# Seven products for the first dense matrix, with its factors streamed from DRAM

## The chip, the cores and the metric

One core of one Trainium2 chip. The time is the device time of one execution in microseconds (us); three runs give a median. A profile of one more execution tells what each engine did.

## The reference

q, k, v are [8, 8, 576, 64]; a decayed causal attention turns them into 4608 tokens of 512 features. A mixture of eight experts follows (each token goes to its best expert: 512 to 1024, relu, 1024 to 512, times its gate). Last comes the dense part, which the change is about:

```python
def _moe2_ref(x, w_in, w_out):      # x 4608 x 512, w_in 512 x 2048, w_out 2048 x 512
    h = x @ w_in
    r = np.maximum(h, 0.0)
    g = r * r
    return (g @ w_out).astype(np.float32)
```

## The kernel before

Matrices are multiplied on TensorE in three terms: each operand is split into a high part and a low rest (`hi`, `lo`), and hi x hi, hi x lo and lo x hi are added in PSUM. A split is a copy on ScalarE (the high part) and a subtraction on VectorE (the rest).

Three stages follow one another. The attention takes the first 200 us or so. The expert part runs over 64 units, eight for each expert, 640 slots an expert: `first(u + 1)` makes 128 hidden features of unit u + 1 (24 matmuls of 320 columns in two halves, whose relu is ScalarE's L718 and whose rest is VectorE's L719), then `second(u)` adds unit u to five accumulators (15 matmuls of 512 columns). While TensorE does this the other engines do, in the order in which the loop over units (L860 on) writes them: SyncE loads the weights seven units ahead, SyncE puts a split of dense weights into DRAM, ScalarE and VectorE split the weights of unit u + 6 (L97, L98; GpSimd does the subtraction in one unit of eight), GpSimd gathers the next expert's tokens, VectorE turns them (L684) and splits them (L689). The dense weights come as 64-bit words. `split_wide` (L127 to L146) takes 512 columns of them apart with seven operations on VectorE and two on ScalarE, five times in eight units; `cw_p` has two buffers for the result, and the transfer to `wd_d` in DRAM is issued two units later. Engines work through their queues in the written order.

The dense part (L916 on) goes over nine blocks of 512 tokens. All 16 tiles of split weights (1 MB each) lie in SBUF: four are loaded late in the expert part, twelve at its end. A step (block b, feature tile f) is `up`: 12 matmuls into one bank; `squares`: relu, square, split, for the step after next; `down`: 12 matmuls of the squares into four accumulators. `fetch` reads a block's rows from `y_d`, `turn` turns and splits them during the block before. The first block begins in halves of 256 columns, since its third and fourth tiles of tokens are scattered to DRAM by the last expert while it starts.

## Time and profile before

| what | value |
|---|---|
| median of 3 runs | 1429.58 us (1426.47 to 1435.66) |
| the profiled execution | 1436.04 us, its span 1434.2 us |
| TensorE busy | 1391.3 us, 97% of the span |
| VectorE, ScalarE, GpSimd busy | 712.5, 435.3, 313.2 us |
| mean granted clock of TensorE | 0.991 of 2.4 GHz |
| mean rate of all transfers | 120 GB/s |

The span runs from the first to the last instruction; the profiled execution's own time is 1.8 us longer. The busy time of an engine is a sum over stages with different limits; the tables by stretch say where it falls. A wait is put down to the signal that came last.

### The profile page before, as it was taken

To read this page: it belongs to the slowest core of one execution; us is meant where nothing else is said; L and a number is where in the kernel's file an instruction comes from. 1 tells how busy PE (TensorE), PEld (TensorE's weight loads), DVE (VectorE), ACT (ScalarE), POOL (GpSimd) and SP (SyncE) were. 2 spreads that over 40 slices of the span, in tenths; PEclk is the share of its full clock that TensorE was granted. 3 is DMA by queue.
4 is the path that set the end of the run, shared out by engine and by line. 5 is a ranking of instruction groups with operands and counts; after the bars stand their busy time and mean duration, and the time that the engine had idled before them with its cause. 6 is when DMAs were issued, how large, how long until landed. Compare 5 with 4: busy or idle time off the path is not lost.

```text
span 1434.2 us, 20323 instructions
## 1 busy us (share of the span) xinstructions
PE 1391.3 (97%) x8217; PEld 1192.2 (83%) x8217; DVE 712.5 (50%) x1187; ACT 435.3 (30%) x764; POOL 313.2 (22%) x277
## 2 busy tenths in 40 slices
PE   7989799998999999999999999999999999999998
PEld 5777688887999999998888888888888888888887
DVE  5667656886888888723323233232333323333222
ACT  1212233443444444422222222222222222222221
POOL 2223246765657557310000000000000000000000
PEclk9999999999999999999999999999999999999999
DMA  8999744765756757538120020200102020020000
GB/s 309 293 298 303 210 131 135 241 226 176 234 186 222 227 185 237 189 134 312 81 59 0 1 59 0 59 1 27 33 0 59 1 57 3 0 59 1 30 0 30
DMA packets 92406, 172.51 MB, mean 120 GB/s; under 512 B 16654, under 2 KB 54030, under 8 KB 86672
## 3 DMA queue, kind: packets, MB, share of 16 engines
q1 hardware_dynamic: 82944, 151.03, 33.3%
q0 software_dynamic: 9360, 20.10, 4.3%
q8 instruction: 66, 1.08, 0.3%
q14 instruction: 36, 0.29, 0.1%
HBM read 125.86 MB, written 46.28 MB: 120 GB/s over the span
## 4 chain that ended last, share of the span: by engine, by line
PE 72%; issue 3%; DMA 1%; POOL 0%; SPq 0%; ACT 0%; POOLq 0%; DVE 0%
PE fl L937 27%; PE fa L959 9%; PE fa L958 9%; PE fa L960 9%; PE l L712 3%; PE l L713 3%; PE l L714 3%; PE acc L737 3%; PE acc L736 3%; PE acc L738 3%; DMA w<-wd_d 1%; DMA y_d<-y,sidx 0%; POOL y_d L227 0%; SPq L633 0%; DMA yi<-y_d 0%
## 5 line engine op out<-in xcount | busy, mean ns | idle before, releaser
L937 PE MATMUL fl<-xt,w 128*128 128x512 f32 (+1 forms) x1776 | 415.3, 383 | 1.5 <-DMA w<-wd_d 1.5
L937 PEld LDWEIGHTS fl<-xt,w 128*128 128x128 f32 x1776 | 327.1, 188 | 67.3 <-issue 1.9
L944 DVE TENSOR_TENSOR fr<-fr 128x512 f32<-128x512 f32 x144 | 99.8, 693 | 401.2 <-ACT fr L942 401.2
L958 PE MATMUL fa<-w,gh 128*128 128x512 f32 x576 | 224.1, 389 | 0.0
L959 PE MATMUL fa<-w,gh 128*128 128x512 f32 x576 | 224.1, 389 | 0.0
L960 PE MATMUL fa<-w,gl 128*128 128x512 f32 x576 | 224.1, 389 | 0.0
L942 ACT ACTIVATE fr<-fl 128x512 f32<-128x512 f32 x144 | 86.2, 599 | 416.0 <-PE fl L937 416.0
L206 POOL DMA_INDIRECT xs<-x_d,qidx x140 | 154.0, 1100 | 44.4 <-issue 42.4
L712 PE MATMUL l<-xt,w 128*128 128x320 f32 (+1 forms) x480 | 150.2, 313 | 8.8 <-DVEq L759 6.2
L713 PE MATMUL l<-xt,w 128*128 128x320 f32 (+1 forms) x480 | 149.8, 312 | 0.0
L948 DVE TENSOR_TENSOR gl<-fr,gh 128x512 fp32r<-128x512 f32 x144 | 99.8, 693 | 100.6 <-ACT gh L946 100.6
L714 PE MATMUL l<-xt,w 128*128 128x320 f32 (+1 forms) x480 | 149.7, 312 | 0.0
L958 PEld LDWEIGHTS fa<-w,gh 128*128 128x128 f32 x576 | 108.1, 188 | 22.5
L959 PEld LDWEIGHTS fa<-w,gh 128*128 128x128 f32 x576 | 108.2, 188 | 22.3
L960 PEld LDWEIGHTS fa<-w,gl 128*128 128x128 f32 x576 | 108.0, 188 | 22.4
L736 PE MATMUL acc<-w,hh 128*128 128x512 f32 x320 | 125.7, 393 | 0.0
L737 PE MATMUL acc<-w,hh 128*128 128x512 f32 x320 | 125.3, 392 | 0.0
L738 PE MATMUL acc<-w,hl 128*128 128x512 f32 x320 | 124.8, 390 | 0.1
L946 ACT ACTIVATE gh<-fr 128x512 fp32r<-128x512 f32 x144 | 91.0, 632 | 109.7 <-DVE fr L944 109.7
L712 PEld LDWEIGHTS l<-xt,w 128*128 128x128 f32 x480 | 90.7, 189 | 12.1 <-issue 6.6
L713 PEld LDWEIGHTS l<-xt,w 128*128 128x128 f32 x480 | 90.7, 189 | 2.4 <-DVE xt L689 0.2
L714 PEld LDWEIGHTS l<-xt,w 128*128 128x128 f32 x480 | 90.7, 189 | 0.0
(140 smaller groups left out, 1511.4 us busy)
## 6 DMA issues: line engine op xcount, KB each, us to landing
raw<-wu SPq DMA_DIRECT2D x62, 512.0 KB, 4.0
in<-att SPq DMA_DIRECT2D x28, 1024.0 KB, 7.9
craw<-wd SPq DMA_DIRECT2D x32, 512.0 KB, 5.6
wd_d<-cw SPq DMA_DIRECT2D x32, 512.0 KB, 6.7
w<-wd_d SPq DMA_DIRECT2D x16, 1024.0 KB, 16.4
x_d<-xr SPq DMA_DIRECT2D x144, 64.0 KB, 5.4
yi<-y_d SPq DMA_DIRECT2D x32, 256.0 KB, 6.0
out<-fo SPq DMA_DIRECT2D x32, 256.0 KB, 2.8
```

The costliest lines, as they stand in the source:

```text
L206: pool.indirect_dma_start(out=xs, out_offset=None, in_=src, in_offset=bass.IndirectOffsetOnAxis(ap=index, axis=0),)
L712: pe.matmul(ps, w[:, 0, k], hi[:, k, cs], start=(k == 0), stop=False)
L713: pe.matmul(ps, w[:, 0, k], lo[:, k, cs], start=False, stop=False)
L714: pe.matmul(ps, w[:, 1, k], hi[:, k, cs], start=False, stop=(k == 3))
L736: pe.matmul(acc[i], hh[:, cs], w[:, 0], start=(f == 0), stop=False)
L737: pe.matmul(acc[i], hh[:, cs], w[:, 1], start=False, stop=False)
L738: pe.matmul(acc[i], hl[:, cs], w[:, 0], start=False, stop=(f == 7))
L937: pe.matmul(ps, w[:, s, k], x[:, k, ts], start=(n == 0), stop=(n == 11))
L944: vec.tensor_tensor(out=gg, in0=r, in1=r, op=ALU.mult)
L958: pe.matmul(acc[i], gh[:, cs], w[:, 0], start=(f == 0), stop=False)
L959: pe.matmul(acc[i], gh[:, cs], w[:, 1], start=False, stop=False)
L960: pe.matmul(acc[i], gl[:, cs], w[:, 0], start=False, stop=(f == 15))
```

## The change

The first dense matrix is multiplied by Strassen's seven products. The 512 contracted features and the 2048 outputs are each cut in two, and so are the tokens: two blocks of 512 form a pair (four pairs), and block 0 is cut into halves of 256. `LEFT` says which quarters of the weights are added for each product, `RIGHT` which quarters of the tokens. A product for one of eight feature pairs (`up`) is 6 matmuls. Products that need one another's sum are added in one bank (1 and 7, 5 and 3 and 6, 4 and 2); three more sums are kept in SBUF. The squares of a pair stay in SBUF (`g`), and `halve` splits them when `down` needs them; `down` keeps its three plain terms.

The left factors are made during the expert part: instead of five splits in eight units there is one item in each unit from 5 to 52, in rounds of six (two narrowings, two sums, two splits), with one `cw_p` buffer in place of two, and the transfer issued in the next unit. They go to 22 tiles of 1 MB in `ws_d`, of which 142 loads are streamed during the dense part through a ring of four (`stream`). The right factors of the next pair are made during `down` of the pair before (`prepare`, two jobs a slot, three in block 0), with GpSimd doing their sums. GpSimd also takes the subtraction of a second unit in eight. Some buffers lie elsewhere in SBUF.

```diff
+LEFT = [
+    (1, "11", ALU.add, "22"), (2, "21", ALU.add, "22"), (3, "11", None, None), (4, "22", None, None),
+    (5, "11", ALU.add, "12"), (6, "21", ALU.subtract, "11"), (7, "12", ALU.subtract, "22"),
+]
+RIGHT = [
+    (1, "11", ALU.add, "22"), (2, "11", None, None), (3, "12", ALU.subtract, "22"), (4, "21", ALU.subtract, "11"),
+    (5, "22", None, None), (6, "11", ALU.add, "12"), (7, "21", ALU.add, "22"),
+]
+ORDER = [5, 1, 4, 7, 3, 2, 6]
+KEPT = [5, 1, 7, 4, 2, 6, 3]
...
-    w_a = scope(ctx, "w_a", 4)
+    xs_p = scope(ctx, "xs_p", 1)
+    xf_p = scope(ctx, "xf_p", 2)
+    w_a = scope(ctx, "w_a", 4, side="right")
...
-    pools["cw_p"] = scope(early, "cw_p", 2, side="right")
+    pools["cw_p"] = scope(early, "cw_p", 1, side="right")
...
-    wd_d = dram.tile([NF, 128, 2, 1024], F32, name="wd_d")
+    ws_d = dram.tile([22, 128, 4, 512], F32, name="ws_d")
...
+    def narrow(raw, tag):
+        t, x = words(raw)
+        a = pools["cv_p"].tile([128, 512], F32, tag=tag, name=tag)
+        vec.tensor_tensor(out=a, in0=t, in1=x, op=ALU.add)
+        return a
...
+        t, x = words(raw)
+        w = pools["cw_p"].tile([128, 4, 512], F32R, tag="cw", name="cw")[:, 0:2]
+        act.activation(out=w[:, 0], in_=t, func=AF.Copy)
+        vec.tensor_tensor(out=t, in0=t, in1=w[:, 0].bitcast(F32), op=ALU.subtract)
+        vec.tensor_tensor(out=w[:, 1], in0=t, in1=x, op=ALU.add)
+        return lambda: sp.dma_start(
+            out=ws_d[14 + v // 2, :, 2 * (v % 2):2 * (v % 2) + 2], in_=w.bitcast(F32)
+        )
...
+    def left_factors(j, x0, x1, part):
+
+        blk = {"11": x0[:, 0:256], "12": x0[:, 256:512], "21": x1[:, 0:256], "22": x1[:, 256:512]}
+        these = KEPT[0:4] if part == 0 else KEPT[4:7]
+        n = len(these)
+        sums = pools["cv_p"].tile([128, 3, 512], F32, tag="cv", name="sums").rearrange("p a (b n) -> p (a b) n", n=256)
+        w = pools["cw_p"].tile([128, 4, 512], F32R, tag="cw", name="cw").rearrange("p k (s n) -> p k s n", s=2)
+        for m, i in enumerate(these[:-1]):
+            _, a, op, b = LEFT[i - 1]
+            vec.tensor_tensor(out=sums[:, m], in0=blk[a], in1=blk[b], op=op)
+        s = blk[LEFT[these[-1] - 1][1]]
+        act.activation(out=w[:, n - 1, 0], in_=s, func=AF.Copy)
+        act.activation(out=w[:, 0:n - 1, 0], in_=sums[:, 0:n - 1], func=AF.Copy)
+        vec.tensor_tensor(out=w[:, n - 1, 1], in0=s, in1=w[:, n - 1, 0].bitcast(F32), op=ALU.subtract)
+        vec.tensor_tensor(
+            out=w[:, 0:n - 1, 1], in0=sums[:, 0:n - 1], in1=w[:, 0:n - 1, 0].bitcast(F32), op=ALU.subtract
+        )
+        k = 7 * j + 4 * part
...
+        def put():
+            for t in sorted({(k + m) // 4 for m in range(n)}):
+                ms = [m for m in range(n) if (k + m) // 4 == t]
+                sp.dma_start(
+                    out=ws_d[t, :, (k + ms[0]) % 4:(k + ms[-1]) % 4 + 1],
+                    in_=w[:, ms[0]:ms[-1] + 1].rearrange("p k s n -> p k (s n)").bitcast(F32),
+                )
+
...
+    stream_of = [t for T in range(5) for t in (*range(14), *(range(14, 22) if T == 0 else 2 * [*range(14, 22)]))]
+
+    def stream(on):
+
+        n = len(ring_q)
+        w = on.tile([128, 4, 2, 256], F32R, tag="w", name="wq")
+        sp.dma_start(out=w.rearrange("p k s n -> p k (s n)").bitcast(F32), in_=ws_d[stream_of[n]])
+        ring_q.append(w)
...
+    def fetch(dst, t, known=True):
         for a in range(4):
-            d = sp.dma_start(out=y[32 * a:32 * a + 32, ts], in_=rows[a][:, ts])
...
+    def factor(i, x1, x2, hi, lo, cs):
+
+
+        _, a, op, b = RIGHT[i - 1]
+        blk = {"11": x1 and x1[:, 0:2], "21": x1 and x1[:, 2:4], "12": x2 and x2[:, 0:2], "22": x2 and x2[:, 2:4]}
+        for ks, h, l in zip((slice(0, 2),) if len(hi) == 1 else (slice(0, 1), slice(1, 2)), hi, lo):
+            h, l = h[:, :, cs], l[:, :, cs]
+            s = blk[a][:, ks]
+            if b:
+                s = xf_p.tile([128, 2, 128], F32, tag="xs", name="xsum")[:, ks]
+                pool.tensor_tensor(out=s, in0=blk[a][:, ks], in1=blk[b][:, ks], op=op)
+            act.activation(out=h, in_=s, func=AF.Copy)
+            vec.tensor_tensor(out=l, in0=s, in1=h.bitcast(F32), op=ALU.subtract)
...
+            x0_t.extend(turn(yi[0][:, t], xf_p) for t in range(2))
...
+            for i in (4, 2):
+                for t in range(2):
+                    factor(i, x0_t[t], None, [x0_c[i, 0]], [x0_c[i, 1]], slice(128 * t, 128 * t + 128))
...
+        work = [(what, j, r) for j in range(8) for what, r in (
+            ("in", 0), ("in", 1), ("sum", 0), ("sum", 1), ("out", 0), ("out", 1))]
...
+            for f_ in put:
+                f_()
+            put.clear()
+            if 4 <= u < 4 + len(work):
+                what, j, r = work[u - 4]
+                if what != "sum":
+                    wide.append(load_wide(2 * j + r, 0 if what == "in" else 1))
...
-                w_q[v] = split_unit(v, raw.pop(v), pool if f == 6 else vec)
+                w_q[v] = split_unit(v, raw.pop(v), pool if f in (5, 6) else vec)
...
-            for j in [j for j in wide if j < wides(u)]:
-                put[min(u + 2, NU - 5)] = split_wide(j, wide.pop(j))
+            if 5 <= u < 5 + len(work):
+                what, j, r = work[u - 5]
+                if what == "in":
+                    made.append(narrow(wide.pop(0), ("ca", "cb")[r]))
+                elif what == "sum":
+                    put.append(left_factors(j, *made, r))
+                    if r:
+                        made.clear()
+                else:
+                    put.append(split_wide(2 * j + r, wide.pop(0)))
...
-                turn(0, 0, 1)
+                first_factors()
...
+        bank_of = {5: "b5", 1: "b1", 4: "b4", 7: "b1", 3: "b5", 2: "b4", 6: "b5"}
+        bank_ps = {"b1": b1_ps, "b4": b4_ps, "b5": b5_ps}
+        steps = [(None, 0)] + [(2 * n - 1, 2 * n) for n in range(1, 5)]
...
+        def up(T, j, i, n):
+            k = 7 * j + KEPT.index(i)
...
+            ps = pt[p, j][:, 0:n]
+            w = ring_q[first_of[T] + k // 4][:, k % 4].rearrange("p s (k n) -> p s k n", k=2)
+            terms = [(c, a, b) for c in range(2) for a, b in ((0, 0), (0, 1), (1, 0))]
+            for m, (c, a, b) in enumerate(terms):
+                pe.matmul(
+                    ps, w[:, a, c], xc[T][i, b][c], start=(i in (5, 1, 4) and m == 0), stop=(m == 5),
+                    skip_group_check=True,
+                )
...
+            def block(b, ps, s):
+                o = g[b][:, j, 0:n]
+                if s is None:
+                    act.activation(out=o, in_=ps, func=AF.Relu)
+                    act.activation(out=o, in_=o, func=AF.Square)
+                else:
+                    vec.tensor_tensor(out=o, in0=ps, in1=s, op=ALU.add)
+                    vec.scalar_tensor_tensor(out=o, in0=o, scalar=0.0, in1=o, op0=ALU.max, op1=ALU.mult)
+
+            if i in (5, 1, 4):
+                keep(f"s{i}", j, ps, n)
+                if all((f"s{m}", j) in sums for m in (5, 1, 4)):
+                    vec.tensor_tensor(out=at("s4"), in0=at("s4"), in1=at("s5"), op=ALU.subtract)
+                    vec.tensor_tensor(out=at("s1"), in0=at("s1"), in1=at("s4"), op=ALU.add)
+                    if j in cut and not cut.discard(j):
+                        vec.tensor_tensor(out=at("s1"), in0=at("s1"), in1=bank("b4"), op=ALU.subtract)
+            elif i == 7:
+                block("11", ps, at("s4"))
+            elif i == 3:
+                block("12", ps, None)
+            elif i == 2:
+                block("21", ps, None)
+                if ("s1", j) in sums:
+                    vec.tensor_tensor(out=at("s1"), in0=at("s1"), in1=ps, op=ALU.subtract)
+                else:
+                    cut.add(j)
+            else:
+                block("22", ps, at("s1"))
+                for m in (1, 4, 5):
+                    sums.pop((f"s{m}", j))
...
+        def halve(T, h, f):
+
+            hi, lo = [pools["cg_p"].tile([128, 512], F32R, tag=f"c{s}", name=f"c{s}") for s in "hl"]
+            if T:
+                parts = [(g["12"[f % 2] + "12"[h]][:, f // 2], slice(0, 512))]
+            else:
+                parts = [(g["12"[f % 2] + "12"[s]][:, f // 2, 0:256], slice(256 * s, 256 * s + 256)) for s in range(2)]
+            for s, o in parts:
+                act.activation(out=hi[:, o], in_=s, func=AF.Copy)
+                vec.tensor_tensor(out=lo[:, o], in0=s, in1=hi[:, o].bitcast(F32), op=ALU.subtract)
+            cg[T, h, f] = hi, lo
...
+                pe.matmul(acc[i], hi[:, cs], w[:, 0], start=(f == 0), stop=False)
+                pe.matmul(acc[i], hi[:, cs], w[:, 1], start=False, stop=False)
+                pe.matmul(acc[i], lo[:, cs], w[:, 0], start=False, stop=(f == 15))
...
+            todo.append(lambda: (load(0), load(1)))
+            for p in range(4):
+                todo.append(lambda p=p: turned(p))
+                for i in ORDER:
+                    todo.append(lambda p=p, i=i: one(p, i))
+                if p + 2 < 4:
+                    todo.append(lambda p=p: load(p + 2))
...
+        head = [(0, "up", j, i) for i in (4, 2) for j in range(2)]
+        slots = []
+        for T in range(5):
+            slots += [(T, "up", j, i) for j in range(8) for i in ORDER if (T, "up", j, i) not in head]
+            slots += [(T, "down", h, f) for h in range(2 if T else 1) for f in range(16)]
...
+        for n in range(4, 8):
+            stream(w_a)
+        for T, _, j, i in head:
+            up(T, j, i, 256)
+        x2 = [turn(yi[0][:, t], x0_p) for t in (2, 3)]
+        for i in (5, 1, 7, 3, 6):
+            for t in range(2):
+                factor(i, x0_t[t], x2[t], [x0_c[i, 0]], [x0_c[i, 1]], slice(128 * t, 128 * t + 128))
+        jobs = []
...
+            for s in slots[m + 2:m + 3] + (slots[m + 1:m + 2] if what == "up" else []):
+                if s[1] == "down" and (s[0], *s[2:]) not in cg:
+                    halve(s[0], *s[2:])
+            if what == "up":
+                up(T, a, b, 512 if T else 256)
+            elif m < len(slots) - 2:
+                if (a, b) == (0, 0) and T < 4:
+                    if T == 0:
+                        x_v.extend(places_of_factors())
+                    jobs = prepare(T + 1)
+                down(T, a, b)
+                if b == 15:
+                    store(T, a)
+                for _ in range(2 if T else 3):
+                    if jobs:
+                        jobs.pop(0)()
+            t = tile_of(T, what, a, b)
+            left[t] -= 1
+            if left[t] == 0 and t >= 4 and t + 4 < len(stream_of):
+                stream(w_a)
```

## Rows read from the trace of the kernel before

**Rows 1.** First page, busy time of an engine (share of span, instructions).
```profile
PE 1391.3 (97%) x8217; PEld 1192.2 (83%) x8217; DVE 712.5 (50%) x1187; ACT 435.3 (30%) x764; POOL 313.2 (22%) x277
```
**Rows 2.** Chain of waits in order of time: start us, us, what.
```profile
641.50 3.19 DMA y_d<-y,sidx
...
645.06 0.43 SPq L633
...
646.01 2.02 DMA yi<-y_d
...
668.69 2.72 PE fl L937 x12
...
674.13 2.72 PE fl L937 x12
```
**Rows 3.** Timeline of TensorE at the dense part's start: start us, us, instructions [idle].
```profile
644.35 5.92 PE L937 MATMUL fl<-xt,w 128*128 128x256 f32 x48
...
662.96 3.01 PE L937 MATMUL fl<-xt,w 128*128 128x512 f32 x12 [1.47 <-DMA w<-wd_d]
```
**Rows 4.** Table of stretches: eight units, one dense block, the branch.
```profile
core 0: us, PE busy (x) PEld busy (x) DVE busy (x) ACT busy (x) POOL busy (x), PEclk, DMA share, GB/s
...
396.60:452.10 55.50, 55.50 (x314) 50.63 (x313) 45.93 (x76) 25.14 (x43) 35.34 (x31) 1.00 0.65 215
750.00:837.00 87.00, 87.00 (x386) 72.06 (x385) 28.59 (x43) 23.20 (x38) 0.00 (x0) 1.00 0.11 25
333.00:345.00 12.00, 10.79 (x56) 10.21 (x57) 7.94 (x13) 3.64 (x6) 9.26 (x10) 0.82 0.33 97
```
**Rows 5.** Timeline of VectorE at the dense part's start.
```profile
641.37 1.31 DVE L648 STREAM_TRANSPOSE yf<-yi 128x512 f32<-128x512 f32 x2
...
649.09 0.76 DVE L656 TENSOR_TENSOR xt<-yf,xt 128x256 fp32r<-128x256 f32 x2 [0.16 <-ACT xt L655]
```
**Rows 6.** Groups of instructions, whole span: busy us, mean ns | idle before.
```profile
L946 ACT ACTIVATE gh<-fr 128x512 fp32r<-128x512 f32 x144 | 91.0, 632 | 109.7 <-DVE fr L944 109.7
...
L298 POOL TENSOR_TENSOR vs<-in,tabv 128x512 f32<-128x512 f32 x36 | 38.0, 1056 | 100.2 <-DMA in<-att 70.6 <-PE stp L335 10.0 <-DMA tabv<-tab_v 5.9
...
L98 POOL TENSOR_TENSOR w<-raw,w 128x1024 fp32r<-128x1024 f32 x11 | 27.0, 2459 | 49.8 <-ACT w L97 43.2 <-DMA x_d<-xr 6.6
...
L395 ACT ACTIVATE ls<-lg 128x256 f32<-128x256 f32 x18 | 6.9, 384 | 21.6 <-PE lg L391 21.5
```
**Rows 7.** Transfers, 653 to 690 us: rate in 40 slices; median landing of issues.
```profile
GB/s 272 176 195 191 215 219 399 425 407 416 416 425 425 425 425 425 416 416 416 416 425 425 425 416 407 407 416 425 425 407 416 425 425 416 416 425 407 345 62 35
...
w<-wd_d SPq DMA_DIRECT2D x12, 1024.0 KB, 19.4
```
**Rows 8.** Timeline of VectorE in the expert part.
```profile
395.93 0.69 DVE L127 SCALAR_TENSOR_TENSOR cx<-cm,craw 128x512 f32<-128x512 f32 x1
...
399.70 0.69 DVE L146 TENSOR_TENSOR cw<-ca,cx 128x512 fp32r<-128x512 f32 x1
400.31 1.22 DVE L98 TENSOR_TENSOR w<-raw,w 128x1024 fp32r<-128x1024 f32 x1
401.45 0.70 DVE L684 STREAM_TRANSPOSE xf<-xs 128x512 f32<-128x512 f32 x1
...
415.26 1.92 DVE L689 TENSOR_TENSOR xt<-xf,xt 128x512 fp32r<-128x512 f32 x1 [0.70 <-ACT xt L688]
```
**Rows 9.** Waits of VectorE from 396.6 to 452.1 us: total, times, longest.
```profile
DVE xt L689 <- ACT xt L688: 3.5, 5, 0.7
DVE hl L719 <- ACT hh L718: 2.4, 3, 1.2
DVE w L98 <- ACT w L97: 1.6, 1, 1.6
```
**Rows 10.** Landing of the 512 KB puts: all 32, then the one at 410.17.
```profile
DMA to landing us min/median/max: 3.1/6.7/10.0
...
DMA to landing us min/median/max: 4.9/4.9/4.9
```

## What the change does to the time, predicted

> **What bounds the kernel now.** I read the first page, then the chain of waits, then tables of stretches, then single engines. The page puts TensorE at 97% of the span [rows 1]. The chain of waits says that this is a true bound: from 663 us to the end it is nothing but TensorE, and 12 matmuls of the first product return every 5.44 us (668.69 to 674.13) [rows 2]. One step of the dense part is 12 matmuls up and 12 down, all 512 columns wide, so one matmul takes 5.44/24 = 0.2267 us. At the head of that stage 48 matmuls 256 columns wide take 5.92 us, with the long tail of the last one 0.12 us each: half the columns cost 53% of the time, so halving a block is nearly free [rows 3]. The one hole there is 1.47 us, waiting for weights. Before 663 us TensorE is full as well: in the eight expert units from 396.6 to 452.1 us it is busy for all 55.5 us, so one unit is 6.94 us. But there VectorE is busy for 45.9 of 55.5 us, while in the dense part it is busy for 28.6 of 87 us [rows 4]. So work that the change takes off TensorE in the dense part is time saved, and work that it adds to VectorE in the expert part may be time lost.
>
> **The change part by part.** *Fewer matmuls.* A pair of blocks takes 32 steps now, 174.1 us. With seven products it takes 7 x 8 x 6 = 336 matmuls up and 384 down, 720 x 0.2267 = 163.2 us. Four pairs save 4 x 10.9 = 43.5 us. Block 0 by itself needs 96 narrow and 144 wide matmuls for its first product now (11.5 + 32.6 us) and waits 1.47 us; with halves of 256 columns it needs 336 narrow ones, 40.3 us: 5.3 us less. Together 48.8 us.
>
> *Start of the dense part.* The rows of the third tile are scattered from 641.50 us, landing after 3.19; the fetch's last issue is at 646.01 and lands after 2.02, at 648.0 [rows 2]; VectorE then turns them. Until then TensorE now has 48 narrow matmuls from 644.35. After the change it has 24 of them (products 4 and 2), 2.9 us, up to 647.3. Product 5 then needs one turn (0.7 us, half of 1.31), one ScalarE copy of 256 columns (0.38) and one VectorE subtraction (0.38, half of 0.76): 649.6 us, a stall of 2.3 us [rows 5, 6]. Products 1, 7, 3 and 6 each need two additions on GpSimd; no row shows one 256 wide. Half of a 512-wide one is 0.53 us, a quarter of a 1024-wide one 0.61 [rows 6]; I take 0.6, as the longer row was taken beside VectorE work. That is 1.2 us a factor against 0.72 us a product: four times 0.48, 1.9 us. So the start costs 4 us (2 if GpSimd runs ahead, 8 if VectorE and GpSimd hold each other up at each factor).
>
> *Inside the dense part.* In block 0 a product lasts 0.72 us and the copy of its bank, 0.38 us and its signals, must end before the next but one adds to that bank: 0 to 0.1 us sixteen times, I take 1 us. When block 0's second product begins, SyncE issues 16 small fetches (0.43 us each [rows 2]), and the turn of the first rows stands in VectorE's queue ahead of the halves that the fourth step needs. Eight issues and a landing are 5.5 us, two turns 1.3, then the queue drains at about the pace of a 2.72 us step: I take 3 us, between 0 and 6. The pairs, with products twice as long and two jobs a step in place of three, get 1 us (0 to 4). VectorE's work of a pair, 56 operations of 0.7 us in the first product and about 56 us in the second, fits in 163 us. Costs inside the dense part and at its start: 9 us, between 2 and 18.
>
> *Weights streamed.* 142 loads of 1 MB replace 16. Twelve of them run at about 420 GB/s in one row, 2.5 us each [rows 7]. A pair uses a tile for 24 matmuls, 5.44 us, and the ring of four gives a load three tiles, 16.3 us. Block 0 uses a tile in 2.9 us and leaves some 8.5 us. The median landing of 19.4 us was with twelve in the queue; here it is two or three. I cost it at nothing: TensorE's work hides it, and the first tiles are issued some 7 us earlier than now because no fetch of block 1 stands ahead of them.
>
> *Expert part: VectorE.* One split of the wide words lasts 4.38 us on VectorE (395.93 to 400.31), and eight units hold five: 21.9 us [rows 8]. After the change every unit from 5 to 52 has one item of work. Of six, two are narrowings (a split less one 0.61 us operation, 3.77), two are splits (4.38), and two form factors: three or two sums of 256 columns, then subtractions of 256 and 768 or 512 columns that wait for ScalarE's copy, 3.0 and 2.15 us from the 0.38 and 0.69 us rows. That is 21.5 us for six units, 28.6 for eight: 6.7 us more. The unit handed to GpSimd takes 1.14 us away (400.31 to 401.45) and gives back 1.23, since a subtraction beside GpSimd's lasted 1.92 instead of 0.69 us (415.26) [rows 8]. The slack is in VectorE's waits: 3.5 us for ScalarE's half of a turn are bound to the work; 2.4 and 1.6 are TensorE's pace and can be eaten, and half a microsecond more [rows 9]. So eight units lack 6.8 - 4.5 = 2.3 us, 48 units 13.8. TensorE lets VectorE fall behind by one second product (15 x 0.2267 = 3.40 us) and half of a unit's other 3.54, 5.2 us, before it waits.
>
> The Trainium skill speaks against the addition of GpSimd work: SBUF — State Buffer, in its part on the shared port pair, says that a VectorE operation with two SBUF inputs and a GpSimd operation that reads SBUF exclude each other for the whole instruction. The 1.92 us row agrees in kind. By the row the moved unit costs VectorE 1.23 us; by the rule up to the whole of GpSimd's 2.4 us [rows 6].
>
> *Expert part: one buffer in place of two.* Each factor or split is written to a tile that the next may overwrite only when its transfer has landed, and the transfer is issued one unit later instead of two. A 512 KB put lands in 3.1 to 10.0 us, median 6.7; one with half a megabyte just ahead of it took 4.9 [rows 10]. The 1 MB put of the first factors has one more half megabyte behind it: between 4.9 and 10.0, I take 5.8. The next factors' copies (0.38 and 0.63, 1.0 us [rows 6]) and last subtraction (0.74 with its signal) then end 0.3 + 5.8 + 1.0 + 0.74 = 7.8 us after the put is ready, where the other work of a unit (55.5 less 21.9 of splits and 4.5 of slack, by eight, 3.6 us) and their own 2.15 would end at 5.8. Eight times 2 us are 16. ScalarE and VectorE stand in that wait with all that is queued behind: the next weights' copy, the turn, the two halves of the hidden layer, on which TensorE waits. A split's copy comes late in its item; with 4.9 us it is hidden in most units, 0.2 us each for sixteen, 3. Less the 5.2 us of lag, and less what falls where VectorE waits anyhow, of 13.8 + 16 + 3 I take 20 us as lost (0 if VectorE's slack is larger than the waits show; 13.8 + 50 + 17 - 5 = 76 if the first puts take 10 and the splits' 6.7).
>
> *Sum.* 48.8 - 9 - 20 = 20 us less. The profiled execution took 1436.04 us (span 1434.2) and would take 1416; it stands 6.5 us above the median of the runs, so against 1429.58 the forecast is 1410 us.
>
> **The rivals.** *The expert part hides its new work* (loss 0 to 8 us): for it speaks that TensorE never waits in eight units today [rows 4], against it the sum above. 1390 to 1400 us. *The puts come late* (slower): if the 1 MB put lands in some 8 to 10 us and the others in the median 6.7, the single buffer paces VectorE: 13.8 + 34 to 50 + 17 - 5 = 60 to 76 us, 1450 to 1466 us; at the median for all 49 us, 1439. It turns slower than before when the expert part loses more than 40 us, and by more than 1% from 54. Against it: puts no longer stand behind a load of words. *The stream is late* (slower): decides from a landing above 16.3 us; at 20 us a tile takes 25.4/4 = 6.4 us, 0.9 us more for 120 tiles: about 110 us more, 1520. Against it, the 2.5 us row. *The shared port holds longer than the row shows*: 1.2 us more per expert for the moved unit, 7 us, and 4 at the start: 1421 us. The page behind it is SBUF — State Buffer of the Trainium skill, as above. A gap in TensorE's work can lower its clock: the stretch 333 to 345 us, behind the expert part's one branch, was granted 0.82 of 2.4 GHz on the mean, part of it at 1.2 [rows 4]. The new start's gaps are shorter, and even so it would cost 1 to 2 us, inside the bounds.
>
> **How the numbers follow.** The sum 0.50 (its own range 1402 to 1421), hidden expert part 0.24, late puts 0.16, late stream 0.03, longer port 0.07. The range that leaves out no more than 2 in 10 is 1388 to 1444. A measurement of this kernel can tell about 1% from no change, 14 us: faster than 1415 are most of the first and all of the second case, 0.60; within 1% the rest of the first, the port and part of the late puts, 0.29; slower than 1444 is 0.11.
>
> **What would show it.** Right: 1344 wide up matmuls and 336 narrow, still 0.2267 and 0.12 us apart; units of 7.2 to 7.6 us instead of 6.94 in the expert part, with TensorE waiting for VectorE's second half of the hidden layer and ScalarE's copies into the factor tile released by transfers; a hole of about 2 us near product 5. Wrong: units still 6.94 us (then 1390), ScalarE waiting 3 us or more for each put (then 1440 and above), or TensorE waiting for weight tiles in the pairs.

## The result

The changed kernel took 1449.26 us (median of 4 runs, 1445.56 to 1451.21) against 1429.71 us of the kernel before: a ratio of 1.0129, 95% interval 1.009 to 1.0168. It is slower by 19.6 us where 20 us less were forecast, and lies above the range. Lengths of stages below run from the start of the first matmul of one stage to that of the next in the profiled execution (the last one to the end of the last matmul); the kernel before had 462.0 us in the expert part and 785.9 us in the dense part.

Beside e1 to e4 and e13 to e18 the kernel before took 1433.81 to 1439.44 us, but beside e5 to e12 it took 1556.22 and 1546.41 us, and in those eight runs TensorE stood 49 to 92 us of the expert part in "issue", which no other trace here shows and no run explains, so only their dense part is read.

| us | before | after | forecast for after |
|---|---|---|---|
| expert part | 462.0 | 498.6 | 482 |
| dense part | 785.9 | 766.9 | 746.1 |
| of it block 0, first and second product | | 54.3, 54.2 | 45.3, 46.5 |
| of it a pair, first product | | 76.2 | 76.2 |
| of it the pairs' second products | | 87.9, 89.1, 89.5, 87.2 | 87.0 and at most 1 for all |

(The first forecast of block 0 is 40.3 + 4 + 1, the second 192 x 0.2267 + 3; the dense part is 785.9 - 48.8 + 9.)

The page of the changed kernel answers [rows 1]: TensorE is busy for less time, and for 94% in place of 97% of the span. The loads of weight tiles land in 4.9 us.

```profile
PE 1364.8 (94%) x8121; PEld 1166.6 (80%) x8121; DVE 868.6 (60%) x1508; ACT 536.0 (37%) x1053; POOL 408.0 (28%) x406
...
wq<-ws_d SPq DMA_DIRECT2D x142, 1024.0 KB, 4.9
```

Busy time by stretch, answering [rows 4] (stretch and its length, then busy us and instructions of each engine, granted clock, share and rate of transfers). The lines are eight expert units, the start of the dense part, the rest of block 0's first product, its second product, and the two products of the first pair.

```profile
396.60:452.10 55.50, 49.99 (x273) 45.43 (x272) 45.84 (x75) 22.41 (x42) 33.04 (x28) 0.94 0.62 199
...
678.00:693.00 15.00, 6.97 (x38) 5.53 (x38) 10.88 (x17) 8.03 (x22) 7.12 (x9) 0.77 0.79 306
693.00:733.00 40.00, 38.58 (x303) 37.62 (x303) 22.08 (x54) 18.42 (x50) 0.00 (x0) 0.96 0.60 216
733.00:786.50 53.50, 47.36 (x191) 36.63 (x191) 32.62 (x79) 22.58 (x69) 16.99 (x28) 0.94 0.68 214
786.50:862.70 76.20, 76.20 (x338) 63.10 (x337) 37.14 (x55) 34.19 (x58) 0.00 (x0) 1.00 0.58 204
862.70:950.60 87.90, 87.35 (x386) 71.90 (x385) 46.88 (x82) 32.60 (x72) 19.49 (x28) 1.00 0.70 229
```

The pair's first product is full to the last tenth. The holes are in the expert part (5.5 of 55.5 us), at the dense start (8 of 15 us) and in block 0's second product (6.1 of 53.5 us). VectorE is busy for only 45.84 of 55.5 us in the eight units, as much as before. It got less done, because about 5 of these 45.84 us are one operation that was held up (below); its waits for others came to 9 us, 8 before.

What TensorE waited for in the expert part (engine, line, what it waited for; us in total, times, longest):

```profile
PE l L780 <- DVE hl L787: 24.1, 16, 5.5
PE l L780 <- DVEq L827: 8.9, 1, 8.9
```

The second line is the branch, 6.2 us before. The first is new: 24.1 us for VectorE's rest of the hidden layer, 2.6 us before. These waits are not the whole loss. The same matmuls also kept TensorE busy for longer. The whole expert part, after and before (columns as above):

```profile
179.57:678.15 498.58, 461.87 (x2551) 414.55 (x2549) 368.84 (x619) 190.58 (x343) 274.25 (x239) 0.98 0.59 194
...
182.34:644.35 462.01, 452.06 (x2550) 410.12 (x2549) 337.60 (x570) 187.30 (x326) 261.82 (x230) 0.99 0.59 195
```

TensorE's idle time grew from 9.95 to 36.71 us, 26.8 us more, and its busy time by 9.8 us; together they are the 36.6 us that the stage lost. The time between the second products of neighbouring units, from the thirteenth on, shows where it falls:

```
before  8.3 6.9 6.9 6.9 6.9 7.0 8.2 6.9 6.9 6.9 6.9 14.7 6.9 6.9 ... (6.9 to the end)
after  10.8 7.5 6.9 8.4 8.2 7.6 8.9 7.9 6.9 8.2 6.9 17.5 6.9 6.9 6.9 8.5 6.9 8.6 6.9 6.9 6.9 6.9 6.9 14.2
        7.0 6.9 6.9 6.9 8.1 7.6 8.3 7.9 7.8 7.9 6.9 7.6 7.7 6.9 6.9 13.2 7.6 6.9 6.9 6.9 6.9 6.9 6.9 8.3 6.9
```

(14.7 and 17.5 hold the branch.) Not every unit is 0.3 to 0.7 us longer, as the prediction's sum spread it: many keep their 6.9 us, some twenty lose 0.6 to 2, one 3.9, and two lose 7.3 and 6.3. The timeline of the first of these two (start, duration, then in brackets the idle time and what ended it):

```profile
425.22 0.20 DVE L286 TENSOR_REDUCE gmx<-glg 128x5 f32<-128x40 f32 x1 [0.30 <-ACT glg L285]
425.45 5.22 DVE L287 TENSOR_SCALAR gmx<-gmx 128x5 f32<-128x5 f32 x1
430.70 0.19 DVE L289 RECIPROCAL gg<-gmx 128x5 f32<-128x5 f32 x1
...
425.86 4.76 POOL L112 TENSOR_TENSOR w<-raw,w 128x1024 fp32r<-128x1024 f32 x2
...
431.21 0.31 PE L782 MATMUL l<-xt,w 128*128 128x320 f32 x1
437.04 0.64 PE L780 MATMUL l<-xt,w 128*128 128x320 f32 x1 [5.51 <-DVE hl L787]
437.47 0.47 PE L781 MATMUL l<-xt,w 128*128 128x320 f32 x1
```

An operation on five elements a partition, part of the gate, which elsewhere has a median of 0.17 us, lasted 5.22 us: as long as GpSimd ran its two subtractions back to back (it had been held up by its own gathers until 425.83). Behind it stood a narrowing, a turn and the two halves of the hidden layer. TensorE then stood for 5.51 us, and the next 12 matmuls took 3.34 us in place of 12 x 0.147 = 1.8, at a granted clock of 0.52 between 437.0 and 440.5. That is the longer busy time: a gap in TensorE's work costs its own length and slower matmuls behind it.

The start of the dense part, answering [rows 3]:

```profile
678.15 3.49 PE L1057 MATMUL b<-xt,wq 128*128 128x256 f32 x24
683.17 0.39 PE L1057 MATMUL b<-xt,wq 128*128 128x256 f32 x1 [1.53 <-ACT xt L722]
684.56 0.86 PE L1057 MATMUL b<-xt,wq 128*128 128x256 f32 x5 [1.01 <-DVE xt L723]
685.60 0.39 PE L1057 MATMUL b<-xt,wq 128*128 128x256 f32 x1 [0.17 <-ACT xt L722]
686.52 1.43 PE L1057 MATMUL b<-xt,wq 128*128 128x256 f32 x5 [0.54 <-DVE xt L723]
692.65 1.65 PE L1057 MATMUL b<-xt,wq 128*128 128x256 f32 x6 [4.70 <-ACT s L1041]
...
686.67 0.89 DVE L723 TENSOR_TENSOR xt<-xsum,xt 128x256 fp32r<-128x256 f32 x1 [0.20 <-ACT xt L722]
687.76 0.88 DVE L723 TENSOR_TENSOR xt<-xsum,xt 128x256 fp32r<-128x256 f32 x1 [0.20 <-ACT xt L722]
...
686.55 0.73 POOL L721 TENSOR_TENSOR xsum<-yf 128x256 f32<-128x256 f32 x1 [0.36 <-DVE xt L723]
687.63 0.72 POOL L721 TENSOR_TENSOR xsum<-yf 128x256 f32<-128x256 f32 x1 [0.36 <-DVE xt L723]
```

GpSimd's sums and VectorE's subtractions take turns: VectorE's 0.42 us operation shows as 0.88, and half a factor comes every 1.085 us, a factor every 2.17. Product 7 may not be added to the bank of product 1 until ScalarE has copied the sum out (L1041), and in ScalarE's queue this copy stands behind the copies of all factors: 4.70 us. Block 0's first product lasts 14.0 us longer than its 336 x 0.12 us: 9.4 are waits (8.0 in these lines, 1.4 behind them), and the other 4.6 are matmuls that took longer than 0.12 us while the clock was low (the last six above: 1.65 us; six in a row at full clock took 0.90 at 731.75 us).

In block 0's second product, SyncE, VectorE and TensorE:

```profile
733.09 12.95 SPq L693 DMA_DIRECT2D yq<-y_d  x16
...
L693 SPq DMA_DIRECT2D yq<-y_d x16: 303/430/648, 733.1 to 745.6; - x16
...
DMA to landing us min/median/max: 1.9/2.0/9.0
...
L303 SPq DMA_DIRECT2D wq<-ws_d x1: 320/320/320, 732.7 to 732.7; - x1
...
DMA to landing us min/median/max: 9.2/9.2/9.2
...
742.85 0.71 DVE L706 STREAM_TRANSPOSE yf<-yq 128x512 f32<-128x512 f32 x1 [6.89 <-DMA yq<-y_d]
...
PE fa L1119 <- ACT ch L1108: 6.0, 4, 4.5
```

The first rows of the next pair are asked for only when this product begins. The 16 issues stretch over 12.95 us, but one of them takes 0.43 us in the median (second line: least, median and most, in ns); between two of them SyncE stood still for 1.6 us and between two others for 3.5, and each time it went on within 0.02 us of the landing of a weight tile (738.14 and 741.92 us). The first fetch was issued at 733.1 us and landed 9.0 us later, at 742.1, just behind the weight tile that had been issued ahead of it (732.7, landed at 741.9). So the rows came late because they stood behind 1 MB tiles in the transfers. The turn, at the head of VectorE's queue, waits 6.89 us for them with the halves of squares behind it. Of the 10.7 us that this product lasts longer than 192 x 0.2267 us, 6.0 are the waits of the last line; the other 4.7 are again slower matmuls behind the gap.

### The profile page after: what moved, and what is told of

It reads as the page before. It is cut to its first block, busy times and chain, and to the rows that moved or that the text cites. A ratio compares the mean times of both kernels' runs of the same rounds, so it can differ in the third digit from the quotient of the medians.

```text
span 1449.4 us, 21516 instructions
## 1 busy us (share of the span) xinstructions
PE 1364.8 (94%) x8121; PEld 1166.6 (80%) x8121; DVE 868.6 (60%) x1508; ACT 536.0 (37%) x1053; POOL 408.0 (28%) x406
## 4 chain that ended last, share of the span: by engine, by line
PE 52%; DVE 9%; DMA 5%; POOL 5%; issue 3%; ACT 2%; SPq 0%; DVEq 0%; ACTq 0%; POOLq 0%
PE b L1057 24%; PE fa L1121 8%; PE fa L1119 8%; PE fa L1120 8%; POOL xs L254 4%; DMA wq<-ws_d 2%; DMA ws_d<-cw 1%; PE l L780 1%; DVE hl L787 1%; PE l L781 1%; PE l L782 1%; DMA xs<-x_d,qidx 1%; PE acc L804 1%; PE acc L805 1%; PE acc L806 1%
## 5 line engine op out<-in xcount | busy, mean ns | idle before, releaser
L1057 PE MATMUL b<-xt,wq 128*128 128x512 f32 (+1 forms) x1296 | 267.9, 364 | 9.4 <-ACT s L1041 5.2
L1057 PEld LDWEIGHTS b<-xt,wq 128*128 128x128 f32 x1296 | 222.9, 190 | 49.3 <-ACT s L1041 5.7
L1119 PE MATMUL fa<-wq,ch 128*128 128x512 f32 x576 | 225.9, 392 | 7.1 <-ACT ch L1108 6.0
L1121 PE MATMUL fa<-wq,cl 128*128 128x512 f32 x576 | 225.8, 392 | 3.0 <-DVE cl L1109 2.9
L1120 PE MATMUL fa<-wq,ch 128*128 128x512 f32 x576 | 225.2, 391 | 0.0
L721 POOL TENSOR_TENSOR xsum<-yf 128x128 f32<-128x128 f32 (+1 forms) x122 | 83.7, 699 | 477.5 <-DVE yf L706 434.2
L780 PE MATMUL l<-xt,w 128*128 128x320 f32 (+1 forms) x480 | 153.5, 320 | 33.1 <-DVE hl L787 24.1
L1109 DVE TENSOR_TENSOR cl<-g,ch 128x512 fp32r<-128x512 f32 (+1 forms) x160 | 103.8, 658 | 134.6 <-ACT ch L1108 131.6
L1108 ACT ACTIVATE ch<-g 128x512 fp32r<-128x512 f32 (+1 forms) x160 | 91.0, 581 | 146.6 <-PE fa L1120 146.6
L1119 PEld LDWEIGHTS fa<-wq,ch 128*128 128x128 f32 x576 | 108.8, 189 | 31.5 <-ACT ch L1108 7.7
L1121 PEld LDWEIGHTS fa<-wq,cl 128*128 128x128 f32 x576 | 108.6, 189 | 28.7 <-DVE cl L1109 6.3
L1120 PEld LDWEIGHTS fa<-wq,ch 128*128 128x128 f32 x576 | 108.8, 189 | 22.6
L780 PEld LDWEIGHTS l<-xt,w 128*128 128x128 f32 x480 | 92.0, 192 | 40.2 <-DVE hl L787 28.7
L1041 ACT ACTIVATE s<-b 128x512 f32<-128x512 f32 (+1 forms) x120 | 66.5, 555 | 106.3 <-PE b L1057 106.3
L781 PEld LDWEIGHTS l<-xt,w 128*128 128x128 f32 x480 | 92.3, 192 | 2.4 <-DVE xt L757 0.2
```

The costliest lines, as they stand in the source:

```text
L780: pe.matmul(ps, w[:, 0, k], hi[:, k, cs], start=(k == 0), stop=False)
L781: pe.matmul(ps, w[:, 0, k], lo[:, k, cs], start=False, stop=False)
L1057: pe.matmul(ps, w[:, a, c], xc[T][i, b][c], start=(i in (5, 1, 4) and m == 0), stop=(m == 5), skip_group_check=True,)
L1109: vec.tensor_tensor(out=lo[:, o], in0=s, in1=hi[:, o].bitcast(F32), op=ALU.subtract)
L1119: pe.matmul(acc[i], hi[:, cs], w[:, 0], start=(f == 0), stop=False)
L1120: pe.matmul(acc[i], hi[:, cs], w[:, 1], start=False, stop=False)
```

## The experiments

The letters in the expectations: A, VectorE's queue runs out of time in the expert part; C, ScalarE and VectorE stand waiting for transfers out of the one buffer; P, GpSimd and VectorE hold each other up. In e1 and e2 the letters mean something else: there A is GpSimd's hold on VectorE, B is too much work on VectorE, and C the single buffer. Where the expert part is unchanged it took 498.6, 500.0 and 501.6 us in three kernels of this study (mean 500.1); gains there are told against this mean.

**e1: GpSimd subtracts in one unit of eight, as before.**

```diff
-w_q[v] = split_unit(v, raw.pop(v), pool if f in (5, 6) else vec)
+w_q[v] = split_unit(v, raw.pop(v), pool if f == 6 else vec)
```

> The changed kernel, but GpSimd takes the subtraction of one unit in eight, as before the change; VectorE gets the other back. The stretch from the first expert matmul to the first matmul of the dense part is 498.5 us in the changed kernel and 462.0 before. Theory A (GpSimd's subtraction holds VectorE up): VectorE's operations lose 18 us less beside GpSimd, and get 7 us of work back, so the stretch falls by about 10 us, to 488, and the two 14 us units are gone. Theory B (VectorE simply has too much work): it rises by about 7 us, to 505. Theory C (the single factor buffer paces it): it stays within 3 us.

1446.51 us against 1433.81, which e1 to e4 share (ratio 1.0082, 1.0057 to 1.0107). The expert part took 493.2 us, 7 less, although VectorE got seven subtractions of 1.14 us back. In VectorE's timeline I summed by how much each operation of the expert part from 200 us on exceeds the median of its line and form (excesses over 0.15 us): 9.9 us before, 28.1 after, 11.2 here. The seven subtractions added to GpSimd (18 in place of 11) thus cost VectorE 28.1 - 11.2 = 16.9 us, 2.4 each, as much as they themselves last (2.4 us each), and took 8 away. Holding is a cause, but 31 us of loss stay, and the two longest units, which were expected to be gone, still took 11.1 and 12.0 us.

**e2: two buffers.** Splits get a buffer of their own, and the rounds go narrowing, narrowing, sum, split, sum, split.

```diff
-("in", 0), ("in", 1), ("sum", 0), ("sum", 1), ("out", 0), ("out", 1))]
+("in", 0), ("in", 1), ("sum", 0), ("out", 0), ("sum", 1), ("out", 1))]
-w = pools["cw_p"].tile([128, 4, 512], F32R, tag="cw", name="cw")[:, 0:2]
+w = pools["cw_p"].tile([128, 2, 512], F32R, tag="co", name="co")
```

> The changed kernel with its work items in the order narrow, narrow, sum, split, sum, split, and a buffer of its own for the splits, so that each buffer is used again two units later (the room comes from a buffer of the branch for overfull experts, which reads into another). Work, order on TensorE and the rest are unchanged. Theory C (the single buffer paces the expert part): ScalarE's waits for transfers before the factor copies, 32 us, are nearly gone and the stretch falls by 15 us or more, from 498.5 to 484 or less. Theory A or B (GpSimd's hold or VectorE's work): the waits are gone too, but the stretch falls by 5 us or less.

1444.86 us (ratio 1.0086, 1.0053 to 1.0119); expert part 494.2 us, 6 less. In the changed kernel ScalarE waited 20.4 us (8 times) and 11.5 us (2 times) for these transfers; here it did not, and most of that came out elsewhere. Theory C carries 6 us, not the bulk.

**e3: each product of block 0's first features right behind its factor.**

```diff
 for i in (5, 1, 7, 3, 6):
     for t in range(2):
         factor(i, x0_t[t], x2[t], [x0_c[i, 0]], [x0_c[i, 1]], slice(128 * t, 128 * t + 128))
+    up(0, 0, i, 256)
```

> The changed kernel, but at the dense part's start each of the five products of the first feature pair is written directly behind its factor, so ScalarE's copies of the banks no longer stand behind the copies of all factors. If the order of ScalarE's queue makes the hole of 4.7 us, the first product of block 0 (54.3 us, of which 40.3 are matmuls) takes 47 to 49 us. If the pace of the factors alone makes it (GpSimd's sum and VectorE's subtraction taking turns, 2.2 us a factor), it stays between 52 and 54.

1456.13 us, block 0's first product 61.1 in place of 54.3 us: against both expectations. ScalarE:

```profile
689.03 0.38 ACT L1041 ACTIVATE s<-b 128x256 f32<-128x256 f32 x1 [7.05 <-DMA y_d<-y,sidx]
689.32 0.71 ACT L722 ACTIVATE xt<-xsum 128x256 fp32r<-128x256 f32 x2
```

The kept sum lies where the last scattered tile of tokens lies, so its copy has to wait for that scatter, and now the factors' copies stood behind it. In the changed kernel the same wait is hidden behind these copies: there the scatter landed at 689.6 us, so even alone in its queue the copy could have come only some 2 us sooner.

**e4: rows fetched early**, before the last features of the first product in place of with the second.

```diff
 if what == "up":
+    if (a, b) == (6, 5) and T < 4:
+        load_rows(T + 1, 0); load_rows(T + 1, 1)
     up(T, a, b, 512 if T else 256)
```

> The changed kernel, but the first rows of the next pair are fetched while its predecessor's first product is in its last two feature pairs, not when the second product has begun. If VectorE's wait for those rows makes the loss there, block 0's second product falls from 54.2 to 45 to 49 us, and those of the pairs by 1 to 2 us each to 87.1. If VectorE and GpSimd holding each other up makes it, block 0's stays at 50 or more.

1443.81 us; block 0's second product 45.3 in place of 54.2 us, the pairs' 87.0, 87.0, 87.1 and 87.2: as expected. But block 0's first product grew to 58.5 us, by one wait:

```profile
PE fa L1119 <- DMA wq<-ws_d: 4.3, 1, 4.3
...
724.78 9.00 SPq L693 DMA_DIRECT2D yq<-y_d  x16
733.88 2.01 SPq L303 DMA_DIRECT2D wq<-ws_d  x4
```

For 9 us SyncE issued the 16 small fetches, and the next weight tiles came behind them. So weights cost nothing only while nothing stands ahead of them in SyncE's queue.

**e8: rows in the gap.** The first pair's rows at feature 1, where transfers stood still because the ring was full (`(6, 5) if T else (1, 5)`).

> The rows of the first pair are fetched when block 0's first group of features is done, near 696 us, where the transfer engines stand idle for 14 us because the ring of weights is full; for later pairs as in the earlier experiment. There the second product of block 0 fell from 54.2 to 45.3 us and the pairs' to 87.0 to 87.2, but the first product of block 0 grew by 4.2 us, with one wait of 4.3 us for a weight tile. If the 16 small fetches then took the place of a weight tile in a stretch where weights use the transfers to nine tenths, the first product is 54 to 55 us here, the rest stays as in the earlier experiment, and the dense part takes 752 to 754 us. If not, the wait for a tile stays.

Block 0 took 54.3 and 46.9 us, the pairs 87.0, 87.0, 88.5 and 87.2; dense part 755.7 us, 11.2 less than after, 2 to 4 more than expected. No wait for a weight tile is left:

```profile
PE b L1057 <- ACT s L1041: 5.2, 2, 4.7
...
PE fa L1119 <- DVE fo L1131: 1.2, 1, 1.2
```

**e6: sums of the right factors on VectorE.** (`pool.tensor_tensor` of `factor` becomes `vec.tensor_tensor`.)

> The sums of the right factors go from GpSimd to VectorE, in the dense start and in every pair. Theory T (GpSimd's sums and VectorE's subtractions take turns, 2.17 us a factor): on VectorE alone a factor is two sums of 0.38 and two subtractions of 0.42 us, 1.6 us, so the four factors take 2.3 us less and block 0's first product falls from 54.3 to 51 to 52.5 us; the pairs' second products (87.9, 89.1, 89.5, 87.2 us), whose stalls are waits for VectorE's half of a split, fall by up to 1 us each. Rival R (what holds the start up is the kept sum, which stands behind all factor copies on ScalarE): 54 us as it is. Rival F (VectorE's added sums delay the splits): the pairs' second products grow by 1 us or more. The expert part stays at 500 us within 2.

Block 0's first product 55.7 us, its second 65.5, the pairs' 95.4, 96.1, 98.0 and 87.2. Rival F for the pairs:

```profile
PE fa L1119 <- ACT ch L1108: 16.7, 13, 5.0
PE fa L1119 <- ACT fo L1133: 8.4, 3, 2.8
```

The sums belong on GpSimd there. The start was 1.4 us longer, not shorter (the thirteen kernels with an unchanged start took 54.2 to 55.3 us): sum, ScalarE's copy and subtraction, written one behind the other on two engines, come to 1.24 us for half a factor against 1.085 (8 x 0.155 = 1.24 us). The start goes by the pace of the factors.

**e5, e9, e13: light narrowings.**

```diff
-t, x = words(raw)
+act.activation(out=m, in_=raw[:, :, 1].bitcast(F32), func=AF.Abs)
 a = pools["cv_p"].tile([128, 512], F32, tag=tag, name=tag)
-vec.tensor_tensor(out=a, in0=t, in1=x, op=ALU.add)
+vec.tensor_tensor(out=a, in0=m, in1=m, op=ALU.add)
```

> Leaves out taking the 64-bit words of the first dense matrix apart: each of the 16 narrowings is one copy on ScalarE and one sum on VectorE (5 operations, some 3.2 us of VectorE work less each, about 50 us in all); its other 32 items and all transfers stay. Theory A (VectorE's extra work fills its queue in the expert part): the stage falls from 498.6 us to 462 to 475. Theory C (ScalarE and VectorE stand waiting for the transfers out of the one buffer): the waits for transfers belong to sums and splits, which stay: 490 to 500. Theory P (GpSimd and VectorE hold each other up in the two units of eight): the two units stay as they are, the stage falls by no more than some 15 us, to 483 or more. The dense part stays at 766.9 us.

> The light narrowings once more, since in the call before TensorE stood 100 us in issue in the expert part whatever the kernel. Leaves out taking the 64-bit words of the first dense matrix apart (5 VectorE operations of each of 16 narrowings, about 50 us of VectorE work). Theory A (VectorE's queue is full in the expert part): the stage falls from about 500 us to 462 to 475. Theory C (transfers out of the one buffer): 490 to 500. Theory P (holding between GpSimd and VectorE): 483 or more.

> The light narrowings a third time, for a chip on which the kernel before takes its 1430 us. Leaves out taking the 64-bit words of the first dense matrix apart (5 VectorE operations of each of 16 narrowings, about 50 us of VectorE work). Theory A (VectorE's queue is full in the expert part): the stage falls from about 500 us to 462 to 475. Theory C (transfers out of the one buffer): 490 to 500. Theory P (holding between GpSimd and VectorE): 483 or more. Where the kernel before stands at 1540 us again, the stage tells nothing.

e5 took 1530.43 us and e9 1524.44; their expert parts are not read.

e13 took 1436.08 us, its expert part 481.4: some 50 us less work on VectorE give 19, fewer than theory A said (25 to 38), and 15.0 us of waits for the rest of the hidden layer stay. Two units still took 10.7 and 11.4 us. So the load counts, but not its mean alone; it matters where the load stands.

**e7, e11, e16: two buffers, and items in seven units of eight.** None in the unit that makes the gate and in which GpSimd subtracts first; the branch goes from unit 18 to unit 20.

```diff
+for n in range(0, 56, 8):
+    work.insert(n, ("none", 0, 0))
```

> The two buffers of the earlier experiment, and the 48 items go into seven units of every eight (none into the unit whose weights GpSimd also subtracts first), so they end by unit 58 instead of 52. Theory A (VectorE's queue is full while items run): the same work over 55 units in place of 48 leaves 7 x 3.6 = 25 us of VectorE time for the rest to fall into; the stage falls from 494.2 us (two buffers alone) to 475 to 485. Theory P (the holding by GpSimd is what costs, item or no item): the unit without an item has the room that the holding takes, and the stage falls by 5 to 10 us. Theory C (transfers): unchanged, 492 to 496. The dense start could lose up to 2 us, since the last transfers into DRAM come six units later.

> Two buffers and items in seven units of eight once more. Theory A: the stage falls from 494.2 us (two buffers alone) to 475 to 485; theory P: 484 to 489; theory C: 492 to 496.

> Two buffers and items in seven units of eight, the rest as changed. Two buffers alone gave 494.2 us. Theory A: spreading the same work over 55 units in place of 48 gives 475 to 487. Theory P: 484 to 490, since the unit that gets no item is one of the two in which GpSimd subtracts. Theory C: 492 to 496.

e7 took 1556.66 us and e11 1552.8; their expert parts are not read. e16 took 1426.94 us, the kernel before 1433.92 beside it (one run each); expert part 477.4 us, 17 less than two buffers alone, and no unit but that of the branch takes over 11 us.

**e18: the spread alone.**

> Items in seven units of eight, none in the one in which the gate is made and GpSimd subtracts first; one buffer as in the changed kernel. If crowding of that unit is the cause by itself, the expert part is 479 to 485 us (17 to 20 off some 500) and the two buffers stay worth 4 to 6. If the spread works only because ScalarE no longer stands in waits for transfers, it is 488 to 495, with those waits still at some 32 us.

1437.35 us, the kernel before 1439.44; expert part 481.2 us, 19 less. TensorE and ScalarE:

```profile
PE l L780 <- DVE hl L787: 9.4, 9, 1.7
...
ACT cw L184 <- DMA ws_d<-cw: 16.6, 6, 4.0
```

Waits for VectorE fall from 24.1 to 9.4 us, the longest from 5.5 to 1.7, while ScalarE's waits for transfers stay (31.4 us with those of the splits, 31.9 in the changed kernel). The crowded unit is the largest single cause, and it acts without the second buffer. One rival remains, since the edit also stretches the same items over 55 units in place of 48: room anywhere might do as much. The traces speak against it. Measured from one second product to the next, against 6.94 us (14.7 for the unit of the branch), the changed kernel loses 22.1 us at the crowded unit and the one behind it and 19.3 at all others; here it loses 3.5 and 17.7. The gain fell where the place was emptied. A kernel that leaves another unit empty was not run.

**e10, e15: the turn of gathered tokens ahead of the subtraction for the next weights.**

```diff
+turned = turn_of(e + 1, f - 2) if e + 1 < NE and 2 <= f < 7 else None
 if v in raw:
     w_q[v] = split_unit(v, raw.pop(v), pool if f in (5, 6) else vec)
...
-transp(e + 1, f - 2)
+transp(e + 1, f - 2, turned)
```

> All work stays. In a unit that turns gathered tokens, VectorE's turn is written ahead of the subtraction for the next weights in place of behind it, so that ScalarE copies the turned tile while VectorE subtracts the weights; now VectorE stands 0.7 us at each of 36 turns (25.6 us in all) waiting for that copy. Theory A (VectorE's queue is full): the stage gains most of these 25 us and falls from 498.6 to 475 to 485 us, and the 0.7 us waits are gone. Theory C (transfers out of the one buffer): these waits lie beside others, no more than 5 us. Theory P: the same holding, 5 us or less. A risk: the turn meets a late gather and holds the subtraction back; then some of the 14.7 us of waits for gathers grows.

> Only the turn is written ahead of the subtraction for the next weights; all work stays. Theory A (VectorE's queue is full, its idle time inside a unit is what is missing): of 36 waits of 0.7 us most go, the expert part falls from about 500 us to 475 to 487. Theory P (holding between GpSimd and VectorE): it stays at 495 or more, and the excess over the median duration of VectorE's operations stays at some 28 us. Theory C (transfers out of the one buffer): 493 or more, with ScalarE's waits for transfers still some 32 us. The dense part stays at 764 to 768 us.

e10 took 1553.99 us; its expert part is not read. e15 took 1445.02 us with 495.7 in the expert part: 4 us less, not 13 to 25, so theory A failed here and P's and C's figures held. VectorE's waits:

```profile
DVE xf L746 <- DMA xs<-x_d,qidx: 28.5, 11, 4.6
DVE xt L759 <- ACT xt L758: 11.1, 16, 1.1
```

The waits for ScalarE's copy fell from 25.6 to 11.1 us, but the turn now meets its gather earlier: 28.5 us in place of 14.7. The risk named beforehand came, and the two nearly cancel.

**e12: all together**, with products between factors, the sums written ahead of the subtractions, and the kept sums moved off the scattered tile.

> Everything that one of the findings speaks for: two buffers, items in seven units of eight, one unit of eight on GpSimd, the turn ahead of the subtraction, rows of the first pair in the gap, later rows early, each product of block 0 right behind its factor with sums on VectorE written one ahead of the subtractions, and the kept sums laid where no scattered tile lies. Theory A: the expert stage is 470 to 480 us (6 from GpSimd, 5 from the buffers, 25 at most from the turn, some from the spread, not adding up wholly), the dense part 748 to 752 (first product of block 0 48 to 51 us, second 46 to 47, pairs 163.2 to 164), so the whole is 1400 to 1412 us, below before. If only theory P or C holds, the expert stage stays at 484 to 490 and the whole at 1412 to 1422.

1541.73 us, against 1546.41 (0.9974, 0.994 to 1.0008). Block 0's first product was 57.9 us, not 48 to 51, its second 46.9 as expected. VectorE and TensorE:

```profile
766.55 0.42 DVE L1087 TENSOR_TENSOR s<-s,s 128x256 f32<-128x256 f32 x1 [1.61 <-ACT s L1047]
...
768.27 2.12 PE L1063 MATMUL b<-xt,wq 128*128 128x256 f32 x6 [2.17 <-ACT xt L1222]
```

With the scatter out of the way, VectorE's sums of products stand between the factors and wait for TensorE and ScalarE, and each product waits for the next factor. Between 766 and 776 us TensorE's granted clock was 0.50, and six narrow matmuls took 2.12 us, where six at full clock took 0.90 in the changed kernel. Products between factors are wrong for a second reason: all three engines stand in one another's queues.

**e14, e17: the findings together**, with all products behind all factors as in the changed kernel; e17 without the turn.

```diff
-factor(i, x0_t[t], x2[t], ...)
+vec.tensor_tensor(out=s, in0=blk[a], in1=blk[b], op=op)
+act.activation(out=h, in_=s, func=AF.Copy)
+rest.append((s, h, l))
+if len(rest) > 1:
+    s, h, l = rest.pop(0)
+    vec.tensor_tensor(out=l, in0=s, in1=h.bitcast(F32), op=ALU.subtract)
```

(and the edits of e1, e8, e15 and e16; only block 0's sums are on VectorE)

> Two buffers, items in seven units of eight, one unit of eight on GpSimd, the turn ahead of the subtraction, the rows of the first pair in the gap and later ones early, and the sums of block 0's right factors on VectorE, each written one ahead of the subtraction before it, with all products behind all factors as in the changed kernel. Where a half factor took 1.085 us with GpSimd and 1.24 us with VectorE's sum and subtraction in turn, it should take about 0.84 us: block 0's first product 54.3 - 8 x 0.245 = 52.3 us, its second 46 to 47, the pairs 163.2 to 164; dense part 752 to 755 us. Expert part, theory A: 470 to 485 us; theories P or C alone: 486 to 492. The whole against the kernel before at 1430 us: 1400 to 1417 by theory A, 1418 to 1426 else. Where the kernel before stands at 1540 us, only the dense part tells.

> The kernel with the findings together, without the turn ahead of the subtraction. It had 466.2 us in the expert part and 753.5 in the dense part. Theory A: the turn carried 10 to 20 us, the expert part is 476 to 486. If the turn carried little, 466 to 472, and the spread with one unit on GpSimd carried the most. The dense part stays within 2 us of 753.5.

e14 took 1409.66 us (4 runs, 1406.64 to 1411.66) against 1436.17: a ratio of 0.9815, 95% interval 0.9783 to 0.9846. It is faster than the kernel before; the changed kernel (1449.26 us) was not run beside it. Expert part 466.2 us, dense part 753.5 (block 0 52.1 and 47.0; pairs 87.0, 87.0, 88.5, 87.2). e17 took 1413.45 us: expert part 471.8, dense 753.6, so the turn is worth 5.6 us. VectorE at e14's start, then TensorE's waits in the expert part:

```profile
657.12 0.42 DVE L1221 TENSOR_TENSOR xsum<-yf 128x256 f32<-128x256 f32 x1
657.47 0.42 DVE L1226 TENSOR_TENSOR xt<-xsum,xt 128x256 fp32r<-128x256 f32 x1
657.92 0.42 DVE L1221 TENSOR_TENSOR xsum<-yf 128x256 f32<-128x256 f32 x1
...
PE l L782 <- DVEq L829: 8.4, 1, 8.4
PE l L782 <- DVE hl L789: 4.0, 4, 2.0
```

Half a factor every 0.80 us: 8 x (1.085 - 0.80) = 2.3 us, and block 0's first product fell by 2.2. That the two agree to a tenth is luck: e17, with the same start, took 53.4 us for it, so the gain is 1 to 3 us. The same 244 us of the expert part in the kernel before, after, and in e14 (columns as above):

```profile
396.00:640.00 244.00, 244.00 (x1372) 222.60 (x1371) 179.35 (x299) 100.10 (x174) 128.50 (x113) 1.00 0.59 198
```

```profile
396.00:640.00 244.00, 227.61 (x1242) 204.93 (x1241) 194.68 (x315) 99.17 (x178) 145.74 (x125) 0.97 0.65 212
```

```profile
396.00:640.00 244.00, 242.65 (x1371) 221.66 (x1371) 199.66 (x347) 105.46 (x189) 128.92 (x116) 1.00 0.65 220
```

VectorE is busier in e14 than in the changed kernel (199.66 against 194.68 us), and TensorE is full. On the mean the work fits; what was lost came from where it stood (and, as e13 shows, less work in the crowded places helps too).

## Why the prediction was wrong, step by step

The measured time lies 39 us above the forecast of 1410: the dense part took 20.8 us more than forecast and the expert part 16.6.

- *Fewer matmuls: right.* 8121 matmuls in place of 8217, and 76.2 us for a pair's first product are 336 x 0.2267 to the tenth. *Weights streamed at no cost: right*; TensorE never waited for a tile in the changed kernel (4.9 us landing). e4 shows what that rested on: SyncE's queue being free. But the stream made the rows of the next pair late, as the next points tell.
- *Start of the dense part, 4 us: mis-sized, about 13 (block 0's first product lost 14 in all).* Three terms failed. The pace of a factor was taken as GpSimd's alone, 1.2 us; with VectorE taking turns it was 2.17, the case that the prediction named and did not take ("8 if VectorE and GpSimd hold each other up at each factor"). And the wait for the copy of the kept sum, behind the factors' copies in ScalarE's queue and at the place of the scattered tile, 4.70 us, was not priced at all. The third is the clock behind the gaps, put at "1 to 2 us, inside the bounds": slower matmuls took 4.6 us here, at a granted clock of 0.77 over these 15 us, 4.7 more in block 0's second product, and 9.8 in the expert part.
- *Inside block 0, 1 us for the first product: right* (1.4 us of idle time behind the start). *3 us for the second: the true figure is 10.7 (8.6 to 10.7 over the kernels that leave it unchanged), above its bounds of 0 and 6*. The step that failed is "eight issues and a landing are 5.5 us". An issue took its 0.43 us; the landing was 9.0 us in place of 2.02, since the rows stood behind weight tiles. Moving them into the gap (e8) gave back 7.3 of it. *Pairs 1 us: about 5.6*, for the same reason, since early rows (e4) took it to 0.
- *Expert part, 20 us: 36.6.* Its terms came to 13.8 + 16 + 3 - 5.2 = 27.6; the last step down to 20, "what falls where VectorE waits anyhow", had no figure behind it. Two steps failed. First, work and slack were compared over eight units, as if they could move between them: "eight units lack 6.8 - 4.5 = 2.3 us". But a queue is in order, and TensorE lets VectorE fall behind by only 5.2 us, as the prediction had worked out itself. The unit that holds the gate, GpSimd's subtractions, a turn and an item went over that, while others kept their slack; taking the item out of it gave 19 us (e18). Second, the price of the moved unit: 1.23 us by the row, 2.4 measured (e1). The rule of the Trainium skill (SBUF — State Buffer, the part on the shared port pair: the loser is blocked for the whole instruction) gave up to 2.4 and is the one that the measurement bears out; here even an operation on 128x5 elements stood for two instructions. The rival of the longer port was thus right in its mechanism and its price (2.4 us of VectorE's time for each subtraction), but taking the seven away gave back only 7 us of the loss; holding hurt most where it met the crowded unit.
- *One buffer, 16 + 3 us:* ScalarE did wait 20.4 us for the first puts, eight times, as forecast with 16. But that wait was mostly not on the path that sets the end: two buffers gave back 6 us. So the rival of the late puts, whose 1439 to 1466 us hold the measured 1449, has the number by luck: the puts of 768 KB and 1 MB landed in 4.9 us in the median, sooner than the 5.8 taken.
- The four edits of the expert part add up: 7 (GpSimd), 6 (buffers), 19 (spread) and 4 (turn) are 36 of the 38 us above 462; together they gave 500.1 - 466.2 = 34. So the edits take back nearly all of the loss, up to about 4 us. Each part is one profiled execution against three that spread over 3.0 us, so the smaller parts (4, 6 and 7) are good to some 2 us, and the parts need not add up exactly.

Not settled: whether an empty place in another unit would do as much. Nor was the kept sum laid elsewhere without products between the factors, so what is left of the 4.7 us wait at the start (3.19 in e14) was not tried.

## What to carry to other kernels

Count an in-order queue unit by unit, not by a mean over eight: the unit that already holds a gate, a turn and another engine's help decides, and one empty place there was worth more than any buffer. Before handing work to GpSimd, price what VectorE loses beside it; here 2.4 us of GpSimd's subtraction cost VectorE 2.4. Count a gap in TensorE's work with the slower matmuls behind it: in the expert part 26.8 us of waits brought 9.8 us more. When a result is needed early, look at everything written ahead of its copy in that engine's queue, and ask for the next block's rows while transfers stand still.

## What was not expected of the hardware

- A VectorE operation on 128x5 elements, 0.17 us in the median, lasted 5.22 us beside two GpSimd subtractions of 4.76 us together.
- After a stall of 5.51 us TensorE's granted clock was 0.52 over 437.0 to 440.5 us, 1.2 GHz for most of it, and 12 matmuls took 1.6 us more than at full clock; in the stuttering start of e12, it was 0.50 for 10 us on end.
- A fetch of 64 KB landed 9.0 us after its issue, 0.2 us behind the 1 MB tile issued just ahead of it; the median of the 16 was 2.0 us. SyncE, with more fetches to issue, stood still for up to 3.5 us meanwhile.
